# 26 block products in place of two times seven: the second MLP product of an attention, Fourier and MLP kernel

## The chip, the cores and the metric

The kernel runs on one core of a Trainium2 chip. The metric is the device time of the whole launch in microseconds (us): 1077.55 in the median of three runs before the change. TensorE, VectorE (DVE), ScalarE (ACT), GpSimd (POOL) and SyncE (SP, which issues most DMAs) each work through a queue of their own in order, and wait for each other by semaphores.

## What is computed

Chunked attention over q, k, v of shape (8, 8, 576, 64), and on its output, seen as x of shape (8, 576, 512), a Fourier mixing and an MLP:

```python
X = np.fft.fft(x, axis=1)
X = np.fft.fft(X, axis=2)
mixed = np.real(X).astype(np.float32)
u = x + mixed
mu = np.mean(u, axis=-1, keepdims=True)
var = np.mean((u - mu) ** 2, axis=-1, keepdims=True)
un = (u - mu) / np.sqrt(var + 1e-06)
ch = np.maximum(un @ w_ch1, 0.0) @ w_ch2
return (u + ch).astype(np.float32)
```

w_ch1 is 512 x 2048, w_ch2 is 2048 x 512 (both arrive as 64-bit floats and are rounded in the kernel); u has 4608 rows. The second product, relu(un @ w_ch1) @ w_ch2, is what the change touches. All arithmetic is fp32.

## The kernel before

**Tiles and groups.** The 576 rows of a batch are held as tiles of 128 rows: two "low", two "high", and one "rest" tile for every two batches. Four tiles make a group; groups 0 to 7 are the batches, group 8 holds the four rest tiles. A group goes through a first product (512 rows x 512 x 2048, Relu, result `h1` held transposed as [128, 16, 512]: 16 blocks of 128 hidden units by 512 rows) and a second product (512 rows x 2048 x 512), `mlp(g)`.

**Plain and halved products.** `up_first`, `up_plain` and `down_plain` are ordinary products: matmuls of 128 x 128 by 128 x 512, 64 for each product. `up_halves` (L1134, groups 2 to 8) and `down_halves` (L1178, groups 1 to 8) cut both factors in two by two blocks and use seven block products instead of eight, with sums of blocks before and after. `NO = 7` products, each in two halves `r` of 128 rows, each of `HF = 8` matmuls with 256 columns (L1200): 112 matmuls. Their results lie in PSUM in `pa` and `pb` (four buffers of the pool `ps_f`), VectorE adds them up (L1207 to L1220) from one partial result to the next in `tmp`, and GpSimd adds the residual (L1212, L1213, L1237). Sums of blocks of `h1` are made by `operands` (L1048: L1050 and L1051 on VectorE, L1052 on GpSimd) while the first product runs, and by GpSimd in L1232 between the products.

**Weights.** Groups 0 and 1 read the whole weights from SBUF (`wa`, `wb`). Their block sums are formed once, by GpSimd, in `keep1` (L992, during group 1's first product) and `keep2` (L1009, at the end of group 0), and written to device memory (`s1`, `s2`) together with the blocks that are used as they are (`keep2_whole`, L1027). From then on slabs are read back for every group by `fetch` (L1037): `wa` holds ten slabs of 256 KB for first products, `wb` three of 1 MB for second products. A fetch is issued once the product that used its place is over:

```python
elif which == 2 and i < NO * (NG - first_of[2]):
    nc.sync.dma_start(out=slab2[i % NS2].rearrange("p m e -> p (m e)"), in_=s2[i % NO])
```

**What lies between the matmuls.** The order of all queues is written out by hand. The main loop runs the groups' products as generators; at each step of some 3.5 us it also takes pieces of the "side" of a batch to come: attention (`attention`: transposes L369, scores L401, softmax L414 and L416, values L451, and copies of single rows by GpSimd, L508), the fold for the Fourier transform (GpSimd, L522 to L548), and `fourier` (matmuls z L672 and mix L791). `ready_at` sets the step by which a side must be over. Its last part falls into the first steps of the second product of the group before: after the mix, ScalarE copies (L796), VectorE forms y (L801, L802) and adds it to the low tile (L808), GpSimd adds it to the high tile (also L808), and VectorE takes the statistics of both (L655, L656), the high one's after GpSimd's addition. A batch with an odd number has a third mix, for a rest tile, ahead of the other two. Groups 3 to 7's batches have these parts in the second products of groups 2 to 6. Later in the second product `normed` (L947, "un"), `turned` (L350, L958) and `combined` (L968 to L971) prepare the next group's first product; `store` (L980 to L989) writes finished tiles out.

Of the kernel before, what the change touches and what calls it, by code (L numbers as in the profile page):

```python
# [8 lines left out]
FP32 = mybir.dt.float32  # L9
# [7 lines left out]
def kernel(  # L17
# [38 lines left out]
    NM = 2  # L56
# [10 lines left out]
    G = 2 * NM  # L67
# [38 lines left out]
    s2 = dram.tile([NO, 128, HF * HM], FP32, name="s2")  # L106
    NS1, NS2, Z1, Z2 = 10, 3, 2 * 2 * 128, HF * HM
    slab1 = [wa[:, i * Z1:(i + 1) * Z1].rearrange("p (k r f) -> p k r f", r=2, k=2) for i in range(NS1)]
    slab2 = [wb[:, i * Z2:(i + 1) * Z2].rearrange("p (m e) -> p m e", m=HF) for i in range(NS2)]
    tt = wa[:, NS1 * Z1:NS1 * Z1 + 3 * 2 * 256].rearrange("p (o k t) -> p o k t", o=3, k=2)  # L110
    tmp = wa[:, NS1 * Z1 + 3 * 2 * 256:NS1 * Z1 + 3 * 2 * 256 + 4 * 256].rearrange("p (i j t) -> p i j t", i=2, j=2)
    xs = wb[:, NS2 * Z2:NS2 * Z2 + HF * 256].rearrange("p (m t) -> p m t", m=HF)
    os_ = xs.rearrange("p (a b) t -> p a (b t)", b=2)
    yall = const.tile([128, 4, 512], FP32, name="yall")
    ys = yall.rearrange("p a (b t) -> p (a b) t", b=2)
# [876 lines left out]
    def keep1(i):  # L992
# [4 lines left out]
        o1, o2, o3, o4 = ((os_ if i % 2 else yall)[:, j] for j in range(4))  # L997
# [11 lines left out]
    def keep2(i):  # L1009

        m = 2 * i
        b11, b12 = w2[:, m:m + 2, 0:HM], w2[:, m:m + 2, HM:DM]
        b21, b22 = w2[:, HF + m:HF + m + 2, 0:HM], w2[:, HF + m:HF + m + 2, HM:DM]
        to = xall[:, 2 * G:2 * G + 4, 0:DM] if i % 2 else yall
        o1, o2, o3, o4 = (to[:, j].rearrange("p (m e) -> p m e", m=2) for j in range(4))
        for out_, in0, in1, op in (
            (o1, b12, b11, ALU.subtract), (o2, b22, o1, ALU.subtract),
            (o3, b22, b12, ALU.subtract), (o4, b21, o2, ALU.subtract),
        ):
            nc.gpsimd.tensor_tensor(out=out_, in0=in0, in1=in1, op=op)  # L1020
            yield
        to = s2.rearrange("o p (m e) -> o p m e", m=HF)
        for o, a in ((1, o2), (2, o1), (3, o3), (6, o4)):
            nc.sync.dma_start(out=to[o, :, m:m + 2], in_=a)
        yield

    def keep2_whole(i):  # L1027

        m = 2 * i
        to = s2.rearrange("o p (m e) -> o p m e", m=HF)  # L1030
        for o, m0, e0 in ((0, m, 0), (4, HF + m, 0), (5, HF + m, HM)):
            nc.sync.dma_start(out=to[o, :, m:m + 2], in_=w2[:, m0:m0 + 2, e0:e0 + HM])

    first_of = {1: 2, 2: 1}
    n_slab = {1: 0, 2: 0}

    def fetch(which):  # L1037
        i = n_slab[which]
        if which == 1 and i < HF // 2 * NO * (NG - first_of[1]):
            pair, o = divmod(i % (HF // 2 * NO), NO)  # L1040
            nc.sync.dma_start(out=slab1[i % NS1].rearrange("p k r f -> p (k r f)"), in_=s1[pair, UP[o]])
        elif which == 2 and i < NO * (NG - first_of[2]):
            nc.sync.dma_start(out=slab2[i % NS2].rearrange("p m e -> p (m e)"), in_=s2[i % NO])
        n_slab[which] = i + 1
# [3 lines left out]
    def operands(h1, m):  # L1048

        nc.vector.tensor_tensor(out=xs[:, m], in0=h1[:, m, hi], in1=h1[:, HF + m, hi], op=ALU.add)  # L1050
        nc.vector.tensor_tensor(out=ys[:, m], in0=xs[:, m], in1=h1[:, m, lo], op=ALU.subtract)  # L1051
        nc.gpsimd.tensor_tensor(out=h1[:, m, hi], in0=h1[:, m, lo], in1=h1[:, m, hi], op=ALU.subtract)  # L1052
# [25 lines left out]
    def up_plain(g):  # L1078
        unT = unTs.pop(g)
        h1 = one_p.tile([128, KF, G * 128], FP32, tag="big", name="h1")  # L1080
        for m in range(KF):
# [10 lines left out]
            if g >= first_of[2] and m > HF:  # L1092
                operands(h1, m - HF - 1)
            yield h1
        if g >= first_of[2]:
            operands(h1, HF - 1)
# [37 lines left out]
    def up_halves(g):  # L1134
# [3 lines left out]
        for pair in range(HF // 2):  # L1138
            pas, pbs = {}, {}
            for turn_, o in enumerate(UP):  # L1140
                w = slab1[((g - first_of[1]) * HF // 2 * NO + pair * NO + turn_) % NS1]
                for r in range(2):
# [17 lines left out]
                    elif o == 3:  # L1160
                        nc.vector.tensor_tensor(out=h1[:, HF + m, hi], in0=dst, in1=a, op=ALU.add)
                        if pair > 0:
                            operands(h1, m - 2)
# [8 lines left out]
                fetch(1)  # L1172
                if turn_ in (1, 3, 5, 6):
                    yield h1
        for m in (HF - 2, HF - 1):
            operands(h1, m)

    def down_halves(g, h1):  # L1178
        pas, pbs = {}, {}
        for o in range(NO):  # L1180
            w = slab2[((g - first_of[2]) * NO + o) % NS2]
            for r in range(2):
                cl, ch = slice(r * 128, (r + 1) * 128), slice(256 + r * 128, 256 + (r + 1) * 128)
                low, high = groups[g][r], groups[g][2 + r]
                olow, ohigh = os_[:, 2 * r], os_[:, 2 * r + 1]
                a, b = tmp[:, r, 0], tmp[:, r, 1]
                if o == 0:
                    pas[r] = ps_f.tile([128, 2, 256], FP32, tag="ff", name="pa")
                if o == 2:
                    pbs[r] = ps_f.tile([128, 2, 256], FP32, tag="ff", name="pb")  # L1190
                dst = (pas, pas, pbs, pbs, pas, pbs, pbs)[o][r][:, (0, 1, 0, 1, 0, 0, 1)[o]]
                lhs = (
                    h1[:, 0:HF, cl], ys[:, :, cl], xs[:, :, cl], h1[:, 0:HF, ch],
                    h1[:, HF:KF, cl], ys[:, :, cl], h1[:, HF:KF, ch],
                )[o]
                k = 2 * o + r
                for m in range(HF):
                    if m == HF // 2 and g + 1 < NG and k in range(5, 5 + 2 * G, 2):
                        turned(g + 1, (k - 5) // 2)
                    nc.tensor.matmul(  # L1200
                        out=dst, lhsT=lhs[:, m], rhs=w[:, m],
                        start=(o in (0, 2) and m == 0), stop=(m == HF - 1), skip_group_check=True,
                    )
                if o == 0:
                    nc.scalar.copy(a, dst)
                elif o == 1:
                    nc.vector.tensor_tensor(out=b, in0=dst, in1=a, op=ALU.add)  # L1207
                elif o == 2:
                    nc.vector.tensor_tensor(out=a, in0=dst, in1=b, op=ALU.add)
                elif o == 3:  # L1210
                    nc.vector.tensor_tensor(out=ohigh[:, HM:DM], in0=dst, in1=ohigh[:, HM:DM], op=ALU.add)
                    nc.gpsimd.tensor_tensor(out=olow[:, HM:DM], in0=b, in1=natural(low)[:, HM:DM], op=ALU.add)  # L1212
                    nc.gpsimd.tensor_tensor(out=ohigh[:, 0:HM], in0=b, in1=natural(high)[:, 0:HM], op=ALU.add)  # L1213
                elif o == 4:
                    nc.vector.tensor_tensor(out=olow[:, 0:HM], in0=dst, in1=natural(low)[:, 0:HM], op=ALU.add)
                elif o == 5:
                    nc.vector.tensor_tensor(out=olow[:, HM:DM], in0=dst, in1=olow[:, HM:DM], op=ALU.add)
                    store(low, olow)
                else:
                    nc.vector.tensor_tensor(out=ohigh[:, 0:HM], in0=dst, in1=ohigh[:, 0:HM], op=ALU.add)  # L1220
                    store(high, ohigh)
                if g + 1 < NG:
                    for j in range(G):
                        if k == 3 + 2 * j:
                            normed(g + 1, j)
                        if k == 5 + 2 * j and j >= 2:
                            combined(g + 1, j - 2)
# [189 lines left out]
```

## Time and profile before

| | |
|---|---|
| three runs, median (lowest, highest) | 1077.55 us (1076.56, 1078.38) |
| profiled execution: its own time | 1076.41 us |
| its span, first to last instruction | 1074.6 us |
| TensorE clock granted | 1.0 |
| group 1: first product, second product begin | 189.8, 254.8 us |
| groups 2 to 8: second products begin | 368.8, 483.0, 596.0, 709.2, 821.8, 923.6, 1022.0 us |
| groups 2 to 8: first products begin | 313.0, 425.5, 540.2, 652.8, 766.5, 875.3, 973.7 us |
| DMA over the whole span | 192.25 MB, 179 GB/s |

An instruction is named by engine and line, with the tile it writes and those it reads. An fp32 matmul stands as two records, and successive records overlap, so it's the distance of their starts that tells the rate. A row of the timeline that ends in `[1.45 <-POOL xall L808]` says that the engine stood idle for 1.45 us before it and that the wait ended with GpSimd's line 808. Rows of stages give a window in us from the start, its length, the busy time of each engine with its number of instructions, the granted clock, the share of the DMA engines' time that was busy, and GB/s.

### The profile page before, as it was taken

Reading aid. Unit: us, or ns where it says so; the run is one execution under the profiler, and the core shown is the slowest. Engines: PE = TensorE matmul, PEld = TensorE weight load, DVE = VectorE, ACT = ScalarE, POOL = GpSimd, SP = SyncE. Lnnn points to the kernel's source line nnn. Section 1 sums busy time; section 2 is a strip of 40 time slices with the busy share of each in tenths; the row PEclk is TensorE's granted clock in tenths of the full one; section 3 lists DMA queues with packets and bytes.
Section 4 is the critical chain, followed back from the end, with each engine's and each line's share of the span. In section 5 each row is a group of like instructions: output and inputs, shape, how many; then the busy total and the mean of one; then the engine's idle time right before and its main releaser. Section 6 shows DMA issues by size and latency. Waiting matters only on the chain.

```text
span 1074.6 us, 19747 instructions
## 1 busy us (share of the span) xinstructions
PE 1054.5 (98%) x7418; PEld 840.0 (78%) x7418; DVE 578.6 (54%) x1269; ACT 311.6 (29%) x732; POOL 330.2 (31%) x475
## 2 busy tenths in 40 slices
PE   8999989999999999999999999999999999999998
PEld 6645444446888888888888888888888888888887
DVE  4798985324567465655565555745664434323411
ACT  4688563123113411323022312331133113101300
POOL 4311017573515240254124321624161401310140
PEclk9999999999999999999999999999999999999999
DMA  8767566598467546892678356945653355436232
GB/s 181 234 184 216 119 195 198 172 300 296 146 192 229 160 144 194 219 243 100 194 203 243 115 167 194 259 152 168 212 168 118 120 184 177 128 141 215 77 118 79
DMA packets 148780, 192.25 MB, mean 179 GB/s; under 512 B 68140, under 2 KB 105004, under 8 KB 141518
## 3 DMA queue, kind: packets, MB, share of 16 engines
q1 hardware_dynamic: 145036, 187.59, 57.8%
q10 hardware_dynamic: 3330, 2.76, 1.0%
q8 instruction: 59, 0.97, 0.4%
q0 software_dynamic: 320, 0.66, 0.3%
q14 instruction: 35, 0.29, 0.1%
HBM read 166.83 MB, written 24.12 MB: 178 GB/s over the span
## 4 chain that ended last, share of the span: by engine, by line
PE 78%; DMA 6%; DVE 4%; POOL 3%; ACT 3%; SPq 3%; issue 2%; POOLq 0%; DVEq 0%; ACTq 0%
PE pb L1200 21%; PE pa L1151 17%; PE pa L1200 16%; PE pb L1151 12%; PE up L1084 2%; PE pt L350 2%; PE up L1064 2%; DMA xall<-in_moe_w_ch_dram 2%; PE mix L791 2%; PE z L672 1%; DMA v<-in_v_dram 1%; PE xp L451 1%; SPq L216 1%; DMA q<-in_q_dram 1%; PE sc L401 1%
## 5 line engine op out<-in xcount | busy, mean ns | idle before, releaser
L1151 PE MATMUL pa<-unT,wa 128*128 128x256 f32 x672 | 159.9, 381 | 1.6 <-DVE wa L1159 1.6
L1151 PEld LDWEIGHTS pa<-unT,wa 128*128 128x128 f32 x672 | 126.2, 190 | 19.4 <-DVE wa L1159 2.0
L1052 POOL TENSOR_TENSOR h<-h 128x256 f32<-128x256 f32 x64 | 55.3, 871 | 231.2 <-DVE wb L1050 138.7
L1200 PE MATMUL pa<-wb,h 128*128 128x256 f32 x512 | 115.7, 380 | 0.0
L1200 PE MATMUL pb<-wb,h 128*128 128x256 f32 x512 | 114.9, 379 | 0.0
L1151 PE MATMUL pb<-wa 128*128 128x256 f32 x448 | 106.6, 381 | 0.0
L1200 PEld LDWEIGHTS pa<-wb,h 128*128 128x128 f32 x512 | 96.0, 190 | 13.0
L1200 PEld LDWEIGHTS pb<-wb,h 128*128 128x128 f32 x512 | 96.3, 190 | 12.6
L1151 PEld LDWEIGHTS pb<-wa 128*128 128x128 f32 x448 | 84.3, 190 | 11.5
L508 POOL COPY xall<-xall 1x512 f32<-1x512 f32 x28 | 17.8, 637 | 147.3 <-DVE xall L468 120.4
L1157 DVE TENSOR_TENSOR wa<-pb,wa 128x256 f32<-128x256 f32 x56 | 23.8, 424 | 69.9 <-ACT wa L1156 69.9
L1200 PE MATMUL pb<-wb,yall 128*128 128x256 f32 x256 | 58.2, 381 | 0.0
L1200 PE MATMUL pb<-wb 128*128 128x256 f32 x256 | 57.7, 379 | 0.0
L1200 PE MATMUL pa<-wb,yall 128*128 128x256 f32 x256 | 57.6, 379 | 0.0
L1105 PE MATMUL dn<-wb,h 128*128 128x512 f32 x128 | 57.5, 597 | 0.0
L1084 PE MATMUL up<-unT,wa 128*128 128x512 f32 x128 | 56.8, 595 | 0.0
L1156 ACT COPY wa<-pa 128x256 f32<-128x256 f32 x56 | 20.9, 372 | 124.0 <-PE pa L1151 81.2
L1151 PE MATMUL pa<-wa 128*128 128x256 f32 x224 | 53.9, 383 | 0.0
L1151 PE MATMUL pb<-unT,wa 128*128 128x256 f32 x224 | 52.9, 379 | 0.0
L1200 PEld LDWEIGHTS pa<-wb,yall 128*128 128x128 f32 x256 | 48.0, 190 | 6.1
L1200 PEld LDWEIGHTS pb<-wb,yall 128*128 128x128 f32 x256 | 47.7, 190 | 6.3
L1200 PEld LDWEIGHTS pb<-wb 128*128 128x128 f32 x256 | 47.6, 190 | 5.9
(265 smaller groups left out, 1766.8 us busy)
## 6 DMA issues: line engine op xcount, KB each, us to landing
wb<-s SPq DMA_DIRECT2D x56, 1024.0 KB
wa<-s SPq DMA_DIRECT2D x196, 256.0 KB
xall<-in_moe_w_ch_dram SPq DMA_DIRECT2D x22, 512.0 KB
q<-in_q_dram SPq DMA_DIRECT2D x96, 112.0 KB
k<-in_k_dram SPq DMA_DIRECT2D x96, 112.0 KB
v<-in_v_dram SPq DMA_DIRECT2D x124, 64.0 KB
yall<-in_moe_w_ch_dram SPq DMA_DIRECT2D x10, 512.0 KB
s<-wb SPq DMA_DIRECT2D x20, 256.0 KB
```

What stands on the lines that cost most here:

```text
L216: eng.dma_start(out=t[p0:p0 + np_], in_=src[b, :, c * CH:c * CH + np_, :].rearrange("h p d -> p h d"))
L350: nc.tensor.transpose(pt[:, j, :], src(j), ident)
L508: nc.gpsimd.tensor_copy(to, from_)
L791: nc.tensor.matmul(out=mix[:, cols], lhsT=zt[:, T], rhs=tab, start=(T == 0), stop=(T == 3), skip_group_check=True,)
L1052: nc.gpsimd.tensor_tensor(out=h1[:, m, hi], in0=h1[:, m, lo], in1=h1[:, m, hi], op=ALU.subtract)
L1064: nc.tensor.matmul(out=up, lhsT=w1[:, kk, m * 128:(m + 1) * 128], rhs=unT[:, kk], start=(kk == 0), stop=(kk == KD - 1), skip_group_check=True,
L1084: nc.tensor.matmul(out=up, lhsT=w1[:, kk, m * 128:(m + 1) * 128], rhs=unT[:, kk], start=(kk == 0), stop=(kk == KD - 1),)
L1105: nc.tensor.matmul(out=dn, lhsT=h1[:, m, s * 128:(s + 1) * 128], rhs=w2[:, m, :], start=(m == 0), stop=(m == KF - 1),)
L1151: nc.tensor.matmul(out=dst, lhsT=w[:, kk, r], rhs=rhs[o][:, kk], start=(o in (0, 1) and kk == 0), stop=(kk == 1), skip_group_check=True,)
L1156: nc.scalar.copy(a, dst)
L1157: nc.vector.tensor_tensor(out=b, in0=pbs[r][:, 0], in1=a, op=ALU.add)
L1200: nc.tensor.matmul(out=dst, lhsT=lhs[:, m], rhs=w[:, m], start=(o in (0, 2) and m == 0), stop=(m == HF - 1), skip_group_check=True,)
```

## The change

- Group 1's second product becomes plain (`first_of` is 2 for both), so slabs for second products start with group 2.
- From group 2 on, the second product is cut into four blocks of rows, four blocks of hidden units and two blocks of columns, and done with 26 block products in place of 32: each has four matmuls of 128 x 128 by 128 x 256, 104 in all. `PRODUCTS` lists them in order: name, the block of `h1` (or a sum of blocks), the slab, the place in PSUM, and the blocks of the result that the partial result is added to or taken from. Small letters are the lower half of one of the four PSUM buffers, capitals the upper half; a letter that comes again adds to what is there.
- `SUMS` lists the sums of blocks of `h1`, all made by GpSimd, 128 x 512 each: six during the first product ("early"), one at the start, and the others right after the product that is their key. Most are made in place, over a block that has been used.
- VectorE adds each partial result from PSUM straight to the result in SBUF (`os_`), the residual with the first one. `operands` and the sums of L1232 and their like are gone.
- There are 24 slabs of 512 KB in `s2`: six blocks of the weights as they are (`keep_raw`, during group 1's first product) and 18 sums, formed by the 23 steps of `MADE` (`keep_made`, two in each step of group 1's second product, every third on GpSimd, else VectorE, in the space of `wa` and `yall`). `wb` holds six slabs; two of the 26 products share a slab with another.
- `keep1` uses one buffer where it used two, in steps of two; the first ten slabs of `wa` are fetched once all sums are made.

```diff
-    NS1, NS2, Z1, Z2 = 10, 3, 2 * 2 * 128, HF * HM
+    NS1, NS2, Z1, Z2 = 10, 6, 2 * 2 * 128, 4 * HM
...
-    slab2 = [wb[:, i * Z2:(i + 1) * Z2].rearrange("p (m e) -> p m e", m=HF) for i in range(NS2)]
+    slab2 = [wb[:, i * Z2:(i + 1) * Z2].rearrange("p (m e) -> p m e", m=4) for i in range(NS2)]
...
+    PRODUCTS = (
+        ("2", "a41", "b11", "c", "+41"), ("13", "a44", "b42", "b", "+42"), ("8", "y0", "s8", "d", "+12"),
+        ("21", "y3", "s21", "c", "+31+32+42"), ("0", "y1", "s0", "d", "+11+21"), ("16", "a22", "b22", "f", "-22"),
+        ("19", "a23", "s19", "d", "+22"), ("15", "a44", "s15", "b", "+41"), ("10", "a31", "s10", "f", "+32"),
+        ("3", "y1", "s3", "b", "-21-22"), ("11", "y3", "b32", "f", "+42"), ("5", "a22", "b21", "C", "+31"),
+        ("24", "a21", "s24", "B", "-32-42"), ("1", "a31", "s1", "D", "-21+41"), ("17", "a13", "s17", "F", "+11"),
+        ("4", "a24", "s4", "C", "-21"), ("22", "a41", "s22", "B", "-21"), ("25", "a32", "s25", "D", "-32"),
+        ("12", "a34", "s12", "F", "+12"), ("20", "a43", "b31", "C", "+41"), ("7", "a11", "s7", "B", ""),
+        ("6", "a14", "s6", "D", ""), ("18", "y2", "s18", "F", "-32"), ("9", "a12", "b21", "B", "-11"),
+        ("14", "y0", "b22", "D", "+12"), ("23", "a33", "s23", "F", "-31"),
+    )
+    SUMS = {
+        "early": "y0=a11-a13 a11=a11-a21 y1=y0-a21 y2=a31-a41 a31=a33-a31 y3=y2-a33",
+        "": "a24=a23+a24", "2": "a41=a22+a42 a22=a21-a22 a21=a41-a21", "13": "a44=a24+a44 a31=a21+a31",
+        "21": "y3=y3+a43", "0": "y1=a44-y1 y1=y1-a23 y0=a12-y0", "16": "a22=a32-a34 a32=a42-a32",
+        "10": "a31=a42-a22 a13=a13+a14 a24=a24+a31 a14=a14+a34 a34=a13+a34 y2=a34+y2",
+        "11": "a43=a44+a43 a12=a41-a12 a12=a12+a13 y0=y0-a32",
+    }
...
-    first_of = {1: 2, 2: 1}
+    first_of = {1: 2, 2: 2}
...
+    def sums(h1, texts):
+
+        for text in texts:
+            out_, a, b, op = parsed(text)
+            out_, a, b = (block_a(h1, x) for x in (out_, a, b))
+            nc.gpsimd.tensor_tensor(out=out_, in0=a, in1=b, op=op)
...
     def down_halves(g, h1):
...
+        sums(h1, SUMS[""].split())
+        for o, (name, a, _, bank, reads) in enumerate(PRODUCTS):
+            w, lhs = slab2[((g - first_of[2]) * NR2 + o) % NS2], block_a(h1, a)
...
+            for m in range(4):
+                nc.tensor.matmul(
+                    out=dst, lhsT=lhs[:, m], rhs=w[:, m],
+                    start=(fresh and not half and m == 0), stop=(m == 3), skip_group_check=True,
+                )
+            for sign_, i, j in zip(reads[0::3], reads[1::3], reads[2::3]):
...
+                nc.vector.tensor_tensor(out=to, in0=base, in1=dst, op=ALU.add if sign_ == "+" else ALU.subtract)
+                left[i] -= 1
+                if left[i] == 0:
+                    store(n, os_[:, i])
+            sums(h1, SUMS.get(name, "").split())
+            fetch(2)
+            if o % 2 == 0:
+                continue
...
+            yield
...
+                if t >= begin[1]:
+                    for _ in range(2):
+                        next(conv1, None)
+                    if n_raw < len(RAW):
+                        keep_raw(RAW[n_raw])
+                        n_raw += 1
+                if t > begin[1] + KF and n_made < len(MADE):
+                    for _ in range(2):
+                        if n_made < len(MADE):
+                            keep_made(n_made)
+                            n_made += 1
+                    if n_made == len(MADE):
+                        for _ in range(NS1):
+                            fetch(1)
+                if t == begin[2]:
+                    for _ in range(NS2):
+                        fetch(2)
```

A step of the main loop now has two of the 26 products, 13 steps a group.

## The prediction

> **What bounds the kernel now.** I read the page first (busy times, then the chain that ended last), then the busy time by stage, then the timeline of TensorE and of the two engines that feed it. The page's first and fourth parts:
>
> ```profile
> PE 1054.5 (98%) x7418; PEld 840.0 (78%) x7418; DVE 578.6 (54%) x1269; ACT 311.6 (29%) x732; POOL 330.2 (31%) x475
> PE 78%; DMA 6%; DVE 4%; POOL 3%; ACT 3%; SPq 3%; issue 2%; POOLq 0%; DVEq 0%; ACTq 0%
> ```
>
> TensorE is the chain almost everywhere. Its busy share says only that matmuls follow each other without holes, so I price matmuls by their spacing. In the second product of group 7, which has little else on TensorE, the timeline has:
>
> ```profile
> 923.59 7.07 PE L1200 MATMUL pa<-wb,h 128*128 128x256 f32 x32
> 930.50 7.07 PE L1200 MATMUL pa<-wb,yall 128*128 128x256 f32 x32
> ```
>
> 32 records start every 6.91 us: 0.216 us a record, two records to an fp32 matmul of 256 columns, so 0.432 us each. Stage by stage (columns: window, length, busy time of PE, PEld, DVE, ACT, POOL, granted clock, DMA share, GB/s), the second product of group 3, the first of group 4, and the second products of groups 7 and 8:
>
> ```profile
> 425.50:483.00 57.50, 56.22 (x501) 48.41 (x494) 36.13 (x83) 16.98 (x38) 21.49 (x41) 1.00 0.90 242
> 483.00:540.20 57.20, 57.20 (x433) 49.81 (x431) 29.16 (x62) 10.93 (x35) 16.89 (x18) 1.00 0.47 151
> 923.60:973.70 50.10, 50.10 (x242) 44.12 (x241) 13.70 (x30) 2.61 (x6) 11.42 (x12) 1.00 0.42 144
> 1022.00:1074.60 52.60, 48.55 (x225) 42.39 (x224) 7.56 (x17) 1.49 (x4) 11.07 (x12) 1.00 0.30 100
> ```
>
> (The first row is the first product of group 3.) TensorE has no hole in a second product, so fewer matmuls there shorten it one for one unless a new wait opens. VectorE works half of it and DMA under half: both have room on average. What matters is when VectorE reads PSUM, so I looked at the stretch where the next batch's Fourier result is added (group 3):
>
> ```profile
> 496.05 3.62 PE L1200 MATMUL pa<-wb,yall 128*128 128x256 f32 x16
> 496.71 0.42 DVE L801 TENSOR_TENSOR y<-y,mix 128x255 f32<-128x255 f32 x1 [1.14 <-ACT y L797]
> 497.74 1.74 POOL L808 TENSOR_TENSOR xall<-y,xall 128x513 f32<-128x513 f32 x1 [11.38 <-DVE y L802]
> 499.51 0.69 DVE L655 BATCH_NORM_STATS2 bst<-xall 128x6 f32<-128x512 f32 x1 [0.25 <-POOL xall L808]
> 500.34 0.39 DVE L1207 TENSOR_TENSOR wa<-pa,wa 128x256 f32<-128x256 f32 x1
> 500.60 5.34 PE L1200 MATMUL pb<-wb 128*128 128x256 f32 x24
> 504.98 1.27 POOL L808 TENSOR_TENSOR xall<-y,xall 128x513 f32<-128x513 f32 x1
> 506.28 0.69 DVE L655 BATCH_NORM_STATS2 bst<-xall 128x6 f32<-128x512 f32 x1 [1.45 <-POOL xall L808]
> 507.11 0.39 DVE L1209 TENSOR_TENSOR wa<-pb,wa 128x256 f32<-128x256 f32 x1
> ```
>
> VectorE's queue holds statistics (L655) that wait for GpSimd's addition (L808). GpSimd does four sums of its own in between, so the second statistics wait 1.45 us. The PSUM read L1209 stands behind them and comes at 507.11, though its matmuls (the first 16 of the row at 500.60) were over near 504.1. Today that costs nothing: the bank isn't written again soon.
>
> **What the Trainium skill says.** "Perfetto Trace Analysis", Identifying the Most-Contended Engine: matmul busy share is no measure of headroom. The trace agrees: PE 98%, yet 7% fewer matmuls of the stage would leave it as full and shorter. "SBUF — State Buffer", Who interferes with whom: a VectorE operation with two SBUF inputs and a GpSimd operation that reads SBUF shut each other out. The trace agrees: L1050, two SBUF inputs, has a mean of 552 ns where L1211 of the same shape from PSUM has 424. "GPSIMD Engine Reference", Elementwise: an fp32 addition costs about 2.6 cycles an element there, 4497 ns for 2048. The trace agrees in size: 1270 ns for 512 (L1002), 1397 in the second product (L1232).
>
> **The change, part by part** (against the profiled execution: 1076.41 us, span 1074.6; the runs' median, 1077.55, is 1.1 more).
>
> *Fewer matmuls.* A second product has 7 x 2 x 8 = 112 matmuls of 256 columns now, and 26 x 4 = 104 after: 8 x 0.432 = 3.45 us less, in groups 2 to 8: 7 x 3.45 = -24.2 us. Group 1 goes to the plain product: 64 matmuls of 512 columns at 0.86 us (eight records of L1084 take 3.44) = 55.0 against 112 x 0.432 = 48.4: +6.6. Net -17.6 if nothing waits.
>
> *GpSimd's sums.* 28 a group on 128x512, six of them during the first product, in place of 8 (L1052), 4 (L1232) and 6 (L1212, L1213, L1237). I take L1232's 1.40 us (same stage), bounds 1.27 (L1002) and 1.60. In groups 7 and 8 the nearest call is product 10 of the list ("3"), which needs the ninth sum: the last Relu comes about 1.2 us after the stage begins, so 1.2 + 9 x 1.40 = 13.8 against TensorE's 9 x 1.73 = 15.5. It fits; at 1.60 it just doesn't (15.6). Cost 0 there.
>
> *PSUM.* Now one place in PSUM is written again by the sixth product of 3.45 us after it, or later. After, it is the second product of 1.73 us after it in the first half ("d", "b", "f"), the third or fourth in the second half. VectorE's reads (30 a group at 0.42 us in place of 28 operations on 256 columns) become something TensorE waits for, and queued ahead of them are the statistics, which wait for L808, which in GpSimd's order stands behind 12 sums. Work it through for group 3, from the start of the second product. TensorE: six products 10.4, the batch's z matmuls 1.5, the mix 1.1, so the mix ends at M = 13.0. GpSimd: 1.2 + 12 x 1.40 = 18.0, then L808 1.53 each: 19.5 (M+6.5), 21.1 (M+8.1). VectorE: first half of the statistics is done at M+3.2 (497.17 to 499.26 in the trace); the second waits to M+6.5, and with 0.87 and two reads of 0.42 product "15" is read at M+8.25. Product "3" reuses its bank and is due at M + 1.73 + 1.73 + 1.1 + 1.73 = M+6.3: 2.0 us of waiting. Then un 0.69, y 0.84, addition 0.69, statistics 0.87 and 0.87, read of "10": M+12.7; "11" reuses that bank, due at M+8.0+2.0: 2.7 more. Groups 3 and 5 lose 4.7. In groups 2, 4, 6 a third mix (1.1 us, no GpSimd) comes earlier and gives GpSimd that time: 1.0 + 2.7 = 3.7. Groups 7 and 8 have no batch behind them: 0. Sum 2 x 4.7 + 3 x 3.7 = +20.5. Bounds: +13 (GpSimd in time, "11" alone waits), +30 (1.60 us a sum, VectorE's SBUF operations shut out as in un's 1.19).
>
> *Weight slabs.* 26 x 0.5 MB in place of 7 x 1 MB a group: 13.6 MB against 7.3. 151 GB/s at a share of 0.47 is 321 GB/s at full share, so 6.3 MB more take 19.6 us: the share goes from 0.47 to about 0.8. A slab's fetch is issued on SP once the product that used its place is over, five products or 8.6 us before it is needed (now 13.8); ahead of it on SP stand loads that wait for VectorE (L203) and stores. I take 4 us in all, a single late slab a group where attention loads run; bounds 0 and +39 (rival below).
>
> *Preparing the weights.* keep2's 16 GpSimd sums leave the end of group 0, where TensorE has holes of 2.0 to 2.3 us at 147 to 170; 23 sums of 1024 columns come in during group 1's second product, on VectorE (about 1.2 us each, an estimate from 692 ns for 512 and 424 for 256) and GpSimd (2.4). VectorE goes from 28.0 busy of 58 us to some 43 of 65, beside TensorE's plain matmuls; the next slabs are fetched some 14 us ahead. I take 0; bounds -2 and +5; without that cover each VectorE sum late shows as 1.2 us.
>
> Sum: -24.2 + 6.6 + 20.5 + 4 = +6.9 on 1076.4: 1083.3, or **1084.5** against the median.
>
> **Rivals.** (1) Faster: VectorE keeps up. If the statistics weren't in the reads' way (GpSimd well ahead of L808), only "11" waits a little or nothing does: 1077.55 - 17.6 = 1060, with 1 us a group 1065. For it: VectorE is half idle. Against: the order of VectorE's queue, in the built kernel too, has the reads behind the statistics; it decides below about 3 us a group (5 x 3.5 = 17.6). (2) Slower still: slabs. A slab each 1.73 us is 304 GB/s. Two windows of 2 us with slabs alone (1030 and 1032) moved 270 and 254, another (1038) 434. At 270 a slab takes 1.94 us and the stage 50.5 instead of 44.9: 7 x 5.6 = 39, under which the waits above lie hidden: 1076.4 - 17.6 + 39 + 1.1 = 1099. For it: share 0.9 in the first products already. Against: full-share windows above 390. (3) Within the measurement: waits of 3 to 4 us a group and no late slab, 1077.
>
> **Chances.** A run tells a difference above about 0.2% (2.2 us). The forecast's mechanism, 3 to 6 us a group: 0.55 (0.05 of it faster, 0.08 within, 0.42 slower). Rival 1: 0.20 (0.19, 0.01, 0). Rival 2 with its milder forms: 0.20 (0, 0.01, 0.19). Anything else, mainly late conversion in group 1: 0.05, slower. Faster 0.24, within 0.10, slower 0.66. The range leaves out about 0.1 on each side: 1066 (low bound of the waits, -24.2 + 6.6 + 13 - 2, and half of rival 1) to 1106 (high bounds of waits and conversion, some slabs late, and rival 2); the forecast's own is 1073 to 1096.
>
> **What would show it.** Right: in groups 2 to 6 the second product lasts about as long as now (57), with two holes on TensorE, ahead of the tenth and eleventh product, ended by VectorE, and statistics waiting for L808's successor by 2 to 3 us; groups 7 and 8 are 3.4 shorter; group 1 6.6 longer. Wrong: second products of 53 us with no hole (rival 1), or holes in groups 7 and 8 ended by a DMA (rival 2); a hole ended by GpSimd's sums would put my 1.40 us wrong.

## The result and the profile after

The changed kernel takes 1134.4 us in the median of four runs (1131.2 to 1136.1), 1.052 times the time before (95% interval 1.049 to 1.055). The forecast, 1084.5 us, had the sign and about an eighth of the size: 6.9 us more were forecast for the profiled execution, and its span grew by 58.1, from 1074.6 to 1132.7. From the page of the changed kernel, its span, the busy times, the DMA total and the chain that ended last:

```profile
span 1132.7 us, 19622 instructions
PE 1061.9 (94%) x7210; PEld 812.1 (72%) x7210; DVE 585.1 (52%) x1275; ACT 306.5 (27%) x716; POOL 440.0 (39%) x518
DMA packets 167117, 234.20 MB, mean 207 GB/s; under 512 B 70092, under 2 KB 106956, under 8 KB 167022
PE 70%; DMA 10%; DVE 7%; POOL 4%; ACT 3%; SPq 3%; issue 2%; POOLq 0%; DVEq 0%; ACTq 0%
```

TensorE's share of the chain fell from 78 to 70%, and what it lost went to DMA (6 to 10), VectorE (4 to 7) and GpSimd (3 to 4). Where, the stages of the changed kernel tell (columns as in the prediction): first and second product of group 3, first of group 4, second products of groups 7 and 8.

```profile
450.10:514.05 63.95, 58.09 (x500) 49.38 (x493) 31.67 (x71) 17.00 (x38) 24.54 (x42) 0.97 0.80 220
514.05:573.15 59.10, 55.35 (x354) 46.77 (x352) 32.26 (x72) 9.74 (x32) 31.79 (x27) 0.97 0.73 224
573.15:637.20 64.05, 59.92 (x530) 50.63 (x529) 28.25 (x66) 17.92 (x43) 23.31 (x39) 0.95 0.73 214
987.10:1033.75 46.65, 46.65 (x225) 41.08 (x224) 18.59 (x44) 1.88 (x4) 27.13 (x22) 1.00 0.85 291
1082.10:1132.70 50.60, 45.06 (x209) 39.33 (x207) 12.53 (x31) 0.70 (x2) 27.00 (x22) 0.97 0.69 229
```

The second product of group 7 is 3.45 us shorter, to the hundredth what eight matmuls less give, at 291 GB/s and without a hole (idle time of TensorE): the slabs alone keep TensorE's pace. Group 8's has 3.5 us less on TensorE, but its tail of last stores grew. What got long are the *first* products, which the change hardly touches. Added up, with the forecast's terms beside them (us):

| | before | after | difference | forecast |
|---|---|---|---|---|
| all ahead of group 2's first product | 313.0 | 317.9 | +4.9 | +6.6 |
| group 2's first product | 55.8 | 70.3 | +14.5 | 0 |
| first products of groups 3 to 6 | 225.0 | 253.6 | +28.6 | 0 |
| second products of groups 2 to 6 | 281.5 | 297.0 | +15.5 | +7.2 |
| groups 7 and 8 | 199.4 | 194.0 | -5.4 | -6.9 |

(7.2 is -17.3 for matmuls, +20.5 for waits, +4 for slabs.) Not all of the 28.6 is waiting. In groups 4 and 6 the first product also has more to do, since the next batch's work is now spread over 29 steps and not 30: 530 records of TensorE in group 4 (third row above), where the kernel before had 472:

```profile
540.20:596.00 55.80, 55.80 (x472) 48.08 (x465) 33.02 (x74) 17.35 (x42) 20.30 (x38) 1.00 0.74 215
```

That is about 1.6 us each: `rows_plain`, below, has no hole in this stage and still takes 57.36 us.

Two things to read more closely. First, the hole ahead of product 11 in group 3, in the timeline of the changed kernel:

```profile
531.55 1.28 POOL L841 TENSOR_TENSOR xall<-y,xall 128x513 f32<-128x513 f32 x1
532.86 0.69 DVE L688 BATCH_NORM_STATS2 bst<-xall 128x6 f32<-128x512 f32 x1 [1.47 <-POOL xall L841]
533.81 0.30 ACT L692 ACTIVATE rstd<-st,eps 128x2 f32<-128x2 f32 x1 [4.99 <-DVE st L689]
534.25 0.36 ACT L829 COPY y<-mix 128x257 f32<-128x257 f32 x1
...
537.59 0.69 DVE L688 BATCH_NORM_STATS2 bst<-xall 128x6 f32<-128x512 f32 x1 [0.21 <-POOL xall L841]
538.41 1.05 DVE L1248 TENSOR_TENSOR wb<-wb,dn 128x256 f32<-128x256 f32 x3
538.86 2.38 PE L1238 MATMUL dn<-wb,yall 128*128 128x256 f32 x5 [2.38 <-DVE wb L1248]
```

The read that frees the bank (L1248) comes after the second mix's statistics (L688), as forecast. They had waited for GpSimd's addition (L841) 1.47 us at the first mix and 0.21 at the second. Between the two, the second mix's copy (L829) stands on ScalarE behind the first mix's rstd (L692), which the prediction had not in its chain. The granted clock of TensorE around that hole (window, length, TensorE's busy time, clock, DMA share, GB/s):

```profile
533.00:536.30 3.30, 3.21 (x15) 1.00 0.65 217
536.30:538.86 2.56, 0.17 (x2) 1.00 0.78 269
538.86:542.30 3.44, 3.44 (x8) 0.52 0.10 42
```

After this hole TensorE runs at half its clock for 3.4 us (the "slow stretch" below): eight records in the time of sixteen, 1.7 us more. Second, the holes in the first products, in the chain of waits of groups 3 and 6 (start, length, what):

```profile
470.27 5.41 DMA q<-in_q_dram
475.68 0.03 issue
475.71 0.05 DVEq L402
475.76 0.05 issue
475.80 0.06 DVE qT L402
...
818.32 5.00 DMA wb<-s
823.32 0.02 issue
823.34 8.96 DMA out_dram<-wb
832.29 0.02 issue
832.31 9.60 DMA k<-in_k_dram
```

TensorE waits for k or q of the next batch (3.4 to 4.8 us of idle time in each of groups 3 to 6, and again the slow stretch). In group 6 the last part of k was issued on SP only when the store of a low tile (`out_dram<-wb`, 128 KB, 9 us) had landed, and that store only when a slab had. In the trace, the DMAs of SP and ScalarE share eight semaphores (101 and 103 to 109), mostly in turn, and each is issued only when the one before it on its semaphore, as a rule the eighth before it, has landed.

### The profile page after: what moved, and what is told of

The parts are those of the page before. It is cut to its first block, busy times and chain, and to the rows that moved or that the text cites. A ratio compares the mean times of both kernels' runs of the same rounds, so it can differ in the third digit from the quotient of the medians.

```text
span 1132.7 us, 19622 instructions
## 1 busy us (share of the span) xinstructions
PE 1061.9 (94%) x7210; PEld 812.1 (72%) x7210; DVE 585.1 (52%) x1275; ACT 306.5 (27%) x716; POOL 440.0 (39%) x518
## 4 chain that ended last, share of the span: by engine, by line
PE 70%; DMA 10%; DVE 7%; POOL 4%; ACT 3%; SPq 3%; issue 2%; POOLq 0%; DVEq 0%; ACTq 0%
PE dn L1238 24%; PE pa L1193 15%; PE pb L1193 11%; PE dn L1147 6%; PE up L1130 5%; DMA wb<-s 3%; PE pt L383 2%; DMA k<-in_k_dram 2%; POOL xall L841 2%; DMA xall<-in_moe_w_ch_dram 2%; PE z L705 1%; SPq L249 1%; PE xp L484 1%; PE sc L434 1%; POOL h L1098 1%
## 5 line engine op out<-in xcount | busy, mean ns | idle before, releaser
L1238 PE MATMUL dn<-wb,h 128*128 128x256 f32 x1064 | 240.9, 380 | 0.7 <-DMA wb<-s 0.7
L1238 PEld LDWEIGHTS dn<-wb,h 128*128 128x128 f32 x1064 | 198.9, 190 | 26.6 <-DVE wb L1248 1.1
L1098 POOL TENSOR_TENSOR h<-h 128x512 f32<-128x512 f32 x126 | 161.2, 1293 | 91.0 <-ACT h L1211 70.2
L1248 DVE TENSOR_TENSOR wb<-wb,dn 128x256 f32<-128x256 f32 x154 | 61.6, 417 | 129.5 <-PE dn L1238 129.5
L1238 PE MATMUL dn<-wb,yall 128*128 128x256 f32 x392 | 101.3, 411 | 19.4 <-DVE wb L1248 11.9
L1147 PE MATMUL dn<-wb,h 128*128 128x512 f32 x256 | 114.6, 597 | 0.0
L1238 PEld LDWEIGHTS dn<-wb,yall 128*128 128x128 f32 x392 | 78.8, 205 | 35.6 <-DVE wb L1248 13.9
L1147 PEld LDWEIGHTS dn<-wb,h 128*128 128x128 f32 x256 | 46.9, 190 | 51.7 <-issue 50.5
L1205 ACT ACTIVATE h<-pa 128x256 f32<-128x256 f32 x56 | 21.5, 384 | 155.3 <-PE pa L1193 155.3
L1210 DVE TENSOR_TENSOR h<-pb,wa 128x256 f32<-128x256 f32 x56 | 23.8, 425 | 73.9 <-PE pb L1193 73.9
L1193 PEld LDWEIGHTS pb<-unT,wa 128*128 128x128 f32 x224 | 43.7, 196 | 20.0 <-issue 13.9
L1199 DVE TENSOR_TENSOR wa<-pb,wa 128x256 f32<-128x256 f32 x56 | 23.4, 423 | 57.3 <-ACT wa L1198 57.3
```

Source lines behind the costliest of these rows:

```text
L1098: nc.gpsimd.tensor_tensor(out=out_, in0=a, in1=b, op=op)
L1147: nc.tensor.matmul(out=dn, lhsT=h1[:, m, s * 128:(s + 1) * 128], rhs=w2[:, m, :], start=(m == 0), stop=(m == KF - 1),)
L1193: nc.tensor.matmul(out=dst, lhsT=w[:, kk, r], rhs=rhs[o][:, kk], start=(o in (0, 1) and kk == 0), stop=(kk == 1), skip_group_check=True,)
L1199: nc.vector.tensor_tensor(out=b, in0=pbs[r][:, 0], in1=a, op=ALU.add)
L1205: nc.scalar.activation(out=h1[:, m, lo], in_=dst, func=ACTF.Relu)
L1210: nc.vector.tensor_tensor(out=h1[:, HF + m, lo], in0=dst, in1=b, op=ALU.add)
```

## The experiments

All times are medians; the kernel before took 1077.9 to 1080.7 beside them.

**Statistics, adder and clock.** `add_on_dve`: GpSimd no longer adds the mix.

```diff
-            eng = nc.gpsimd if kind(n) == HI else nc.vector
-            eng.tensor_tensor(out=x[:, 0:w], in0=y[:, 0:w], in1=x[:, 0:w], op=ALU.add)
+            nc.vector.tensor_tensor(out=x[:, 0:w], in0=y[:, 0:w], in1=x[:, 0:w], op=ALU.add)
```

> The mix's addition to the high tile is done by VectorE and no longer by GpSimd, so that the statistics wait for no engine but VectorE. Theory of the prediction (reads of PSUM stand behind statistics that stand behind 12 GpSimd sums): the holes of 2.5 us before the product 11 and of about 1 us before product 3 go in groups 2 to 6, with the slow stretch of 1.7 us after each longer one: 4.3 to 6 us a group, about 24 us less, near 1110. Rival (VectorE is itself too full of statistics, un and y at that place): the hole keeps 1.5 us or more and the gain is under 10 us.

It took 1146.8 us, 12 more. The hole in group 3's second product, from its timeline:

```profile
541.26 2.53 DVE L840 TENSOR_TENSOR xall<-y,xall 128x512 f32<-128x512 f32 x2
545.32 1.05 DVE L1247 TENSOR_TENSOR wb<-wb,dn 128x256 f32<-128x256 f32 x3
545.76 1.65 PE L1237 MATMUL dn<-wb,yall 128*128 128x256 f32 x3 [3.77 <-DVE wb L1247]
```

The two additions take VectorE 2.5 us in sequence, and the hole grew from 2.4 to 3.8. This doesn't clear GpSimd, because the edit did two things: it took away the waits for GpSimd (1.7 us in group 3), and it gave VectorE 3.5 us of new work ahead of the read (an addition of 1.75 us after each mix). By these two the hole of group 3 should grow by 1.8 (an estimate); it grew by 1.4. And in the changed kernel the first mix's statistics waited for GpSimd in all five groups, 2.79 us in group 2 and 1.45 to 1.47 in the others, and the chain that ended last runs through GpSimd's sums. From that chain, the hole of group 2:

```profile
404.37 1.27 POOL h L1098
405.63 1.24 POOL xall L841
406.90 0.70 DVE bst L688
...
409.88 1.72 POOL xall L841
411.62 0.71 DVE bst L688
412.53 0.32 DVE wb L1248
```

At the second mix GpSimd had been idle for 3.0 us and waited for y (L835). So the forecast's cause was at work at the first mix and not at the second, and VectorE's own queue makes the rest. `stats_later` leaves the addition where it was and moves the statistics behind the next two products' reads:

```diff
-            means(ns)
+            if b >= 3:
+                pending.append(ns)
+            else:
+                means(ns)
...
             if o % 2 == 0:
                 continue
+            while pending:
+                means(pending.pop(0))
```

> In the second products of groups 2 to 6 the statistics of a mix stand in VectorE's queue behind the PSUM reads of the two products after it and no longer ahead of them. Theory A (the reads come late because VectorE has the next batch's y, addition and statistics in its queue, whoever does the addition): the hole of 2.5 us before product 11 falls below 1 us, and with it goes the stretch of 3.4 us in which the matmuls after it start every 0.43 us instead of 0.216: 3.4 us a group, 17 in all, near 1117. Theory B (the reads are late whatever the order, since the second mix's y waits for ScalarE): the hole keeps over 2 us, 1134.

1117.9 us, near theory A's 1117. From its timeline, group 3:

```profile
533.50 1.08 DVE L1253 TENSOR_TENSOR wb<-wb,dn 128x256 f32<-128x256 f32 x3
533.96 1.35 PE L1243 MATMUL dn<-wb,yall 128*128 128x256 f32 x5 [0.69 <-DVE wb L1253]
534.49 0.69 DVE L690 BATCH_NORM_STATS2 bst<-xall 128x6 f32<-128x512 f32 x1
```

The read now stands ahead of the last statistics, and TensorE waits 0.7 us. In groups 2, 4 and 6, where theory A had said below 1 us, 1.4 to 1.6 stay; in group 2 the chain still begins with GpSimd's sums. No slow stretch follows any of the five holes. The second products of groups 2 to 6 are 19.5 us shorter together; the first products of groups 3 to 6 are 5.2 longer. `filled_hole` asks what the idle itself costs:

```diff
+            if name == "11" and g + 2 < NG:
+                fill = ps_t.tile([128, 512], FP32, tag="pt", name="fill")
+                for _ in range(8):
+                    nc.tensor.matmul(out=fill[:, 0:128], lhsT=ident, rhs=ident, start=True, stop=True)
```

> Eight matmuls of 128x128 by 128x128 on constants (0.22 us each, 1.7 us in all, result not used) ahead of product 11 in groups 2 to 6, where TensorE waits 2.5 us. The wait for VectorE ends when it ended. If the slow matmuls after a hole are due to TensorE having stood idle for over 2 us: idle time falls to 0.8 us, the slow stretch goes, 1.7 us a group, 8.5 in all, near 1126. If they are due to anything else at that place: 1134, the same slow stretch.

```profile
537.95 1.95 PE L1240 MATMUL fill<-ident 128*128 128x128 f32 x16
540.51 1.99 PE L1242 MATMUL dn<-wb,yall 128*128 128x256 f32 x8 [0.60 <-DVE wb L1252]
```

With work of no use in the hole, the eight records after it take 1.99 us and not 3.66, and the slow stretch is gone in all five groups, so the idle time was its cause. The second products of groups 5 and 6 are each 1.7 us shorter, just that stretch. All in all it gained 5 and not 8.5 us (1129.5): the second products of groups 2 to 6 fell by 12.8, and the first products of groups 2 to 6 grew by 6.5. What is saved before a wait for a transfer is waited there.

**Bytes, number and order of the transfers.** `half_bytes` fetches half of each slab:

```diff
-            nc.sync.dma_start(out=slab2[i % NS2].rearrange("p m e -> p (m e)"), in_=s2[slab])
+            nc.sync.dma_start(
+                out=slab2[i % NS2][:, 0:2].rearrange("p m e -> p (m e)"), in_=s2[slab][:, 0:Z2 // 2])
```

> Each slab of a second product is fetched by half only (256 KB of 512, the same number of DMAs in the same places of SP's queue); the products use what lay in the other half, so part of the second product is computed from wrong weights. Bytes theory (the DMA engines are full when the next batch's q and k are to land): the first products of groups 3 to 6 lose their holes and fall from 62 to 64 us to the 55 to 57.5 of before, 28 us in all, and the long hole of group 2 shrinks by about 4: near 1102. Queue theory (q and k are issued late on SP, behind 26 slab fetches that each wait for a product and for one of eight places for DMAs under way): nothing moves but group 2's hole, 1130. Second products keep their holes of 2.5 us in both.

1109.8 us. First products of groups 3 and 4:

```profile
445.21:509.10 63.89, 57.97 (x499) 49.30 (x494) 31.59 (x71) 16.99 (x38) 24.53 (x42) 0.97 0.79 210
567.08:624.44 57.36, 57.36 (x530) 48.78 (x529) 28.18 (x66) 17.90 (x43) 23.32 (x39) 1.00 0.70 203
```

Groups 4 and 6 recover, 3 and 5 don't (nor does group 2, 70.2 us), so the two kinds have different last causes. Of the 24.6 us gained, 11.1 are in the second products, which no longer wait for slabs. `pace_30` goes for the others:

```diff
-                    due = min(sizes[cur], (t - t0) * sizes[cur] // (t1 - t0))
+                    more = int(cur > 1 and t1 - t0 == 29)
+                    due = min(sizes[cur], (t - t0 + more) * sizes[cur] // (t1 - t0 + more))
```

> A batch's side has 29 steps of the main loop where it had 30, because a second product has 13 and not 14; here the share of the side that is due is counted as in the kernel before, so that its pieces stand at the same steps of the first product as there. If the holes of 5 us in the first products of groups 3 and 5 come from q loads that the new pacing puts behind two more slab fetches: they fall to the 1.3 us of before, 6 us a group with the slow stretch, 12 in all, near 1122. If SP's backlog makes them, nothing changes beyond 3 us.

1124.2 us: first products of groups 3 and 5 fall from 63.9 and 63.6 to 59.7 and 59.3, those of 4 and 6 to 57.7 and 57.3. But 9.5 of the 19.6 us come back in the second products: as the work that was moved back there, and as slabs that land late (12.8 us of idle time where it was 5.2). `slab_pairs` moves the same bytes with 13 DMAs a group (each 1 MB, `wb[:, j * Z2:(j + 2) * Z2]` from one row of `s2`):

> The same bytes in half as many DMAs: two slabs that follow each other lie together in device memory and are fetched by one DMA of 1 MB, once the second of the two products that used the place is over. Queue theory: up to 28 us less, near 1106, with q and k issued as early after the start of a first product as in the kernel before (2 to 13 us). Bytes theory: unchanged, 1134, first products of 62 to 64 us.

1136.5 us. Groups 4 and 6 recover as with half the bytes (57.4, 56.9), and about as much is lost to slabs that are fetched a product later. `slabs_on_act` (`nc.scalar.dma_start` for the slabs):

> The slabs of second products are issued from ScalarE's queue, so that q, k and v on SP no longer stand behind them; the same bytes, the same number of DMAs. If SP's order makes q and k late: the holes of 3.4 to 5 us in the first products of groups 3 to 6 shrink below 2, 20 us less, near 1114. If the DMA engines do: they stay, 1134 or above, as ScalarE's Relu and copies now stand behind fetches.

1147.9 us: holes of 2.7 to 4.7 us stay, and ScalarE's own work now waits. Taking slabs out of SP's instruction order isn't enough; they still share the eight semaphores. The reverse test, `before_more_bytes`, loads the kernel *before*:

```diff
             nc.sync.dma_start(out=slab2[i % NS2].rearrange("p m e -> p (m e)"), in_=s2[i % NO])
+            nc.sync.dma_start(out=spare[i], in_=s2[i % NO])
```

> The kernel before, with 1 MB more copied in device memory after each slab of a second product (7 MB a group, about what the change adds; nothing reads it). If the bytes alone delay q, k and slabs: first products of groups 3 to 6 get holes of 3 to 6 us, 20 to 30 us in all, near 1103. If the number and order of DMAs matter more: within 5 us of before, 1078 to 1083.

1125.4 us, 46.6 more. Second product of group 3, first of group 4:

```profile
505.90:563.20 57.30, 57.30 (x434) 49.87 (x432) 29.16 (x62) 10.92 (x35) 16.86 (x18) 1.00 0.63 224
563.20:628.90 65.70, 58.78 (x468) 50.00 (x465) 32.78 (x74) 17.17 (x42) 20.30 (x38) 0.92 0.77 230
```

This is the change's mark without the change: the second product keeps its 57.3 us, the first product after it grows by 10, though the DMA engines were only 0.63 busy. Half as many bytes, `before_half_more`:

> The kernel before, with 0.5 MB more copied in device memory after each slab of a second product (3.7 MB a group, half of the run with 1 MB, which took 46.6 us more). If every MB delays q, k and slabs by its own time on the DMA engines: half of it, 23 us, near 1101, holes of about 2 us in the first products. If only what goes beyond the time that the second product leaves counts (a threshold): under 10 us, 1079 to 1088.

1100.8 us, 20 more than the 1080.7 beside it. That is near proportion (23 would be half of 46.6); these two points show no threshold.

**Through what.** In `before_more_bytes` SP stood 10 us at q loads, for the landing of a store, while the engines moved under 100 GB/s for 4 us (567 to 571), and then k took 8.3 us to land. The chain of waits there:

```profile
562.71 7.47 DMA out_dram<-wb
570.18 0.02 issue
570.20 0.33 SPq L204
...
574.75 8.33 DMA k<-in_k_dram
```

The store in this chain is one of a high tile (64 KB, from ScalarE's queue), which runs on all 16 DMA engines. The stores of low tiles do not. The Trainium skill, "DMA: Bandwidth & Descriptors", Why a DMA increments its semaphore by 16 and not by 1: a DMA runs on the largest number of engines up to 16 that divides the slowest dimension of both sides. The output side of a low tile's store is [2, 32, 512] (odd and even rows, reversed): 2 engines. The trace agrees. The DMA view of the changed kernel from 580 to 584, when k of group 4's hole waits behind such stores (40 slices of 0.1 us; the digit is the busy share of the 16 engines in tenths):

```profile
DMA  9947724514312211111111111111114692976997
GB/s 471 369 164 307 307 82 164 225 61 164 123 61 102 82 41 62 61 41 41 61 61 41 41 61 61 41 41 61 61 41 164 225 348 82 369 266 143 369 492 307
```

For 1.6 us the share is a tenth and 41 to 62 GB/s move: two engines' worth. The semaphore updates in the trace show what that does to k. A low tile's store has three, one soon after it is issued and two at its landing, where each q, k or slab has 16. Of the 16 of the last of k's four loads, issued at 584.66, fourteen had come by 587.57, and the other two came at 594.15 and 594.26. From 320 us on, 53 transfers have their last two updates over 3 us after the fourteenth. So a load over all 16 engines waits for the two that the stores use.

Four kernels write these rows in plain order, so in other places of the output:

```diff
-                to = out[b, t0 + 1:t0 + CH + 1, :][::-1].rearrange("(i r) d -> r i d", r=2)[::-1]
-                nc.sync.dma_start(out=to, in_=o[r0:r0 + CH])
+                nc.sync.dma_start(out=out[b, t0 + 1:t0 + CH + 1, :], in_=o[r0:r0 + CH])
```

> The changed kernel, with the rows of the low tiles written to the output in the order in which they lie in the tile and not reversed and interleaved (the output has these rows in other places; the same bytes, the same DMAs). Theory: a low tile's store, whose output side has a slowest dimension of 2, runs on 2 of the 16 DMA engines and takes 9 to 13 us to land; it holds a place in SP's eight and the two engines, and q, k and slabs wait behind it. Then the holes of 3.4 to 5 us in the first products of groups 3 to 6 shrink below 2.5 and group 2's of 10.7 shrinks too: 15 to 30 us less, 1105 to 1119. Rival (the volume of slabs alone): within 5 us of 1134.

> The kernel before with 1 MB more copied after each slab (46.6 us more), now with the low tiles' rows stored in plain order (rows of the output in other places). Theory of the slow stores (the copies cost time because q and k wait behind stores that land late): 20 us less or more, 1105 or below. Volume alone: 1120 to 1126.

> The kernel before with the low tiles' rows stored in plain order (rows of the output in other places). It has one hole of 1.3 us in group 3's first product that a q load ends: 0 to 3 us less in either theory, 1075 to 1079.

`rows_plain` took 1096.3 us, 38 less. First products of groups 3 and 4:

```profile
445.16:501.39 56.23, 56.16 (x499) 48.27 (x494) 31.67 (x71) 17.00 (x38) 24.55 (x42) 1.00 0.91 246
560.15:617.51 57.36, 57.36 (x531) 48.77 (x530) 28.19 (x66) 17.93 (x43) 23.39 (x39) 1.00 0.86 235
```

All slabs at full size, and the holes are gone: 26.2 of the 28.6 us of groups 3 to 6. A low tile's store now has 16 updates and lands in 4.7 us (median; 9.3 before), and no transfer has its last two updates over 3 us late. Group 2's first product keeps 65.3 us. `more_bytes_rows_plain` took 1102.5 us, 22.8 less than with slow stores; `before_rows_plain` 1073.5, 5 us under the one beside it (ratio 0.9935 to 0.9966) where 0 to 3 were expected. So the slow stores are not the whole cause: with rows in plain order the copied bytes still cost 29.0 us of 46.6, now in holes of 2.4 to 4.3 us that end with slabs of the first product (`wa`), and the change still costs 22.7. These kernels also write contiguous rows where the original skips. For how long a store itself takes, that wasn't parted from the number of engines; that the others wait for two engines, the updates show.

**Group 1 and group 2.** `before_plain_1` is the kernel before with `first_of = {1: 2, 2: 2}` and its first slabs fetched at `begin[2]`. (Some sums of `keep1` lie over the last weights of `w2` there, so group 1's second product uses wrong values.)

> The kernel before with group 1's second product plain and nothing else of the change (the first three slabs of second products are then fetched when group 2's first product begins). Forecast's term: 6.6 us more, 1085. If the plain product also makes group 2's hole of 10.7 us (all stores of group 1 at its end, then 3 MB of slabs at once): 12 us on top, near 1097.

1092.1 us: group 2's first product begins 5.0 us later and takes 67.5 us in place of 55.8. The plain product alone makes most of what the change costs there (11.7 of 14.5 us): all stores of group 1 come at its end, then 3 MB of slabs at once. `spread_first` fetches the six slabs one by one:

```diff
-                if t == begin[2]:
-                    for _ in range(NS2):
-                        fetch(2)
+                if begin[2] < t <= begin[2] + 2 * NS2 and (t - begin[2]) % 2 == 0:
+                    fetch(2)
```

> Group 2's first six slabs are fetched at every second step of its first product, and not all at once at its start. If the burst of 3 MB ahead of the slabs of the first product makes the hole of 10.7 us there, the hole goes with the slow stretch after it: 12 us less, near 1122. If the row stores of group 1 ahead of them on SP make it, the hole stays within 3 us of its length: 1132.

1132.4 us: the hole of 10.6 us became four, 7.2 in sum, now for q, k and slabs of the first product. Both expectations were too simple.

**Together.**

> Statistics behind the reads and the side paced by 30 steps, together. If the two costs are independent: 16.5 and 10 us less than the 1134 of the changed kernel, near 1108. If what is saved in a second product is lost in the first product after it, because slabs, q and k come at the pace of the DMA engines or of SP: 1114 or more.

> Statistics later, side paced by 30 steps, first six slabs spread over group 2's first product; whole slabs. If group 2's hole of 10.7 us and the delays of groups 3 to 6 are separate costs, the spreading gains here what it didn't alone: 1112.8 less some 8, near 1105. If what is spread only shifts the wait to q and k, as it did alone (70.3 to 67.9 us): 1109 to 1113. In neither case under the 1078 of before.

> Statistics later, side paced by 30 steps, first slabs spread, and slabs fetched by half (half of each slab is what lay there before, so part of the second product is computed from wrong weights): all causes named so far, taken away. If they are the whole of the 75 us between the 1060 of matmuls without waits and the 1134 measured: near 1068, second products of groups 2 to 6 of 53 to 54 us and first products of groups 3 to 6 of 56 to 58. If another wait stands behind them: over 1080.

> The run with statistics later, side paced by 30 steps and first slabs spread (1110.4), with the low tiles' rows stored in plain order (rows of the output in other places). Theory of the slow stores: 10 to 25 us less, 1086 to 1100. Volume of slabs alone: within 4 us of 1110.

They took 1112.8, 1110.4, 1075.8 and 1089.9 us. (Their edits are those above, put together as the expectations say.) `later_pace` says that the gains don't add up (21.6 of 26.7). `later_pace_spread` gained 2.4 more and not 8. In `all_half` first products of groups 3 to 6 take 55.3 to 55.9 us and second products of 2 to 6 51.6 to 55.6: what was named is nearly all there is. It is 8 us over the 1068 expected; group 2's first product alone keeps 10 us (65.7). `all_rows_plain` leaves slabs that land 0.9 to 2.6 us late in the second products. No kernel with rows and weights in their places came under the one before. Storing the reversed rows over more engines in their right places wasn't tried.

## Why the prediction was wrong

- *Fewer matmuls*: right. Group 7: 3.45 us less.
- *GpSimd's sums*: 1.40 us were taken, the mean is 1.29; none ended a hole in groups 7 and 8.
- *PSUM*: the place of the holes was right, and the sum near (16.0 us for 20.5, counted from when the next matmul was due, 0.16 us more than the idle time in the timeline). Ahead of product 11, 2.7 was forecast and 2.5 came. Ahead of product 3, 1.0 was forecast in groups 2, 4 and 6, where 1.0 to 1.4 came, and 2.0 in groups 3 and 5, where nothing came. That reads behind statistics cause it is shown by `stats_later`. GpSimd's sums have a part in it, by the waits of 1.45 to 2.79 us at the first mix; how much, no run shows alone. The size for product 11 was in part luck: in group 3 GpSimd's first addition ended 4.7 us after the mix and not 6.5, the second 9.4 and not 8.1, because it waited for a y that stood behind rstd. The two errors nearly cancel.
- Not in the working: the clock after a hole, 5 x 1.7 us. The Trainium skill, "TensorE: Matmul & The Clock Gate", Part 1: The HAM clock gate, has it (half the clock after an idle window of about 3.4 us). Here shorter holes were enough: it followed those of 2.0 to 2.4 us of idle time in the second products, but not one of 2.6 us at 438 nor one of 2.4 at 149. In `rows_plain` it did not follow the same holes of 2.4 us in groups 5 and 6, and in `pace_30` not one of 3.1 at 565. So there is no firm limit; the page says that the windows run freely.
- *Weight slabs* is the step that failed. "I take 4 us in all, a single late slab a group": late slabs in the second products of groups 2 to 4 did cost 5.7, with one slow stretch 7.3. But I asked only when a slab is late for its own product. The larger cost lies in the next stage, where q and k, issued one tile ahead, stand behind slabs and stores on SP and on the engines: 28.6 us, of which some 3 are the work that the pacing moved there. I named the loads and stores on SP ahead of a slab and not the loads behind it. The kernel before showed the edge: a hole of 1.3 us in group 3's first product, ended by a q load, at a DMA share of 0.90. Rival 2 had the cause and a size (39 us), but for another place: TensorE waiting for slabs in second products, groups 7 and 8 too.
- *Group 1* at +6.6: 4.9 came ahead of group 2 (its second product took 8.1 us more, its first 3.7 less; why, stays open). The burst after the plain product, up to 14.5 us in group 2, wasn't in it.
- *Preparing the weights*: no late conversion seen, as taken.

## What to carry to other kernels

Before bytes are added to a stage, list every transfer that is issued behind them, to the end of the next stage, and which of them was already just in time. A mean DMA share of 0.63 in the stage that got the bytes didn't rule out 46.6 us in the next ones, for it says nothing of a queue in which one slow store holds up what follows. Count how many engines each store uses. And a hole on TensorE of 2 us or more may bring slow matmuls after it (here 1.7 us, mostly but not always), and is to be priced with them.

## What the hardware showed beyond that

Stores of 128 KB on two engines took 6.2 to 12.8 us to land (28 stores, median 9.3), about twice as long as a slab of four times the size (median 4.5). What was spread over all 16 engines behind them had fourteen parts in time and two up to 7.8 us later. And in the kernel before each MB copied (read and written) in the second products cost 0.7 to 0.8 us (20 and 46.6 us for 29.4 and 58.7 MB) although no second product was stopped.
